# A schedule's leads by block, and second-layer weights left until block 3

## The chip, the cores and the metric
One core of a Trainium2 chip runs the whole program. The metric is the device time in microseconds (us), the median of several runs. TensorE does the matrix products and takes its instructions in order; ScalarE and VectorE move results out of the accumulators and do all arithmetic by element, each in its own order; SP issues the transfers between memories, also in order, and waits with the whole queue where one transfer has to wait.

## What is computed
Three stages follow each other: a scan with decay over 768 positions of 4 x 8 heads, and two layers of two products each.
```python
def _attn_ref(x, a, B, C):          # chunks of 32 positions
    ...
        L = np.exp(cum[:, :, :, None] - cum[:, :, None, :])
        L = L * causal
        M = np.einsum('bhin,bhjn->bhij', Cc, Bc) * L
        y[:, :, sl] = M @ xc + (Cc @ state) * np.exp(cum)
        state = decay_full * state + sum_j(Bc[j] * xc[j] * decay_from_j)
    ...
def _moe_ref(x, w_in, w_out):       # first layer, 3072 x 256 -> 2048 -> 256
    h = x @ w_in
    return np.maximum(0.01 * h, h) @ w_out
def _moe2_ref(x, w_in, w_out):      # second layer, the same sizes
    h = np.maximum(x @ w_in, 0.0)
    return h * h @ w_out
```
(The lines of the scan are shortened.) The result is 3072 tokens x 256 numbers in float32.

## The kernel before
**The scan** runs over 12 pieces of 256 positions, counted from 0 here as in the code; three pieces in a row are one sequence of the batch. `scan_a` (L356) and `scan_b` (L401) are generators that emit a step at each `yield`. For one piece they make, in this order: scales of its inputs (for later sequences from sums of squares over `all` loads, L307), the half-precision parts `him`, `ch`, `xh`, `cl`, `kmx`, `xl`, two decay scans `le` (L229, L234), the products S from `kbd` (32 columns wide, L388), `mkh` and `mkl`, the products Y from `xbh` and `xbl` (48 columns wide, L417 to L419), the state scan `stt` (L251), its halves `shl` and their transpose `t` (L426 to L430), the products Y from `sbd` (32 columns, L438), and at last `yh` and `yl` (L447, L448), which are the first layer's input. `kbd`, `xbh`, `xbl` and `sbd` are block-diagonal operands, each put together by four transfers that SP issues (`diag`, L348).

**The first layer** (class `One`) runs over 9 blocks, `BLOCKS`: six of one piece, three of two pieces. A block has 16 column groups of 128 hidden units; a step takes two of them (`hmm` into `hp`, 12 products of 256 columns), `act` makes `g` in two halves, and `omm` adds a step's share to the output `oo` two or three steps later (12 products). Block 0 works in plain single precision on weights as they come (`raw`); block 1 and later use each weight and input as a sum of two parts, three products for one.

**Weights** come as 64-bit floats. A chunk is loaded into `wst` (L122), turned into 32-bit numbers by two ScalarE instructions (L131, L134) and two VectorE ones (L142 and L147 or L151), and split into two parts, one instruction on each engine (L173, L174). There are 16 chunks for the first layer (`w1i`, `w1o`) and 16 for the second (`w2i`, `w2o`), in the order of the list `wq`. `raw_step` (L186) moves chunks on in blocks before and during block 0, `w_one` (L194) does one step of one chunk afterwards; the variable `acc` says how often (L721).

**The order.** One loop (L698) goes through all steps of the nine blocks; a step counts as two columns in the position `pos`. After each step, `stages_to(due(pos + 2))` (L708) emits as many steps of the scan as are due there: stage k holds the first half of piece k and the second half of piece k - 1, and `starts` (L673) says which stage has to be reached how many columns ahead of each block. Between, the due stage rises by `RATE` per column. The build then sets each engine's instructions in an order that follows the emission but isn't equal to it; that order is fixed in the program.

**The second layer** (class `Two`, L555) follows with six groups of two pieces, 512 columns a product.

Of the kernel before, what the change touches and what calls it, by code (L numbers as in the profile page):

```python
# [38 lines left out]
LAG2 = 2  # L39
W_AHEAD = 4  # L40
RATE = 1.4 / KO
LEAD = 4
NSTEP = 15
APART = 3
PRE = 8
# [9 lines left out]
def ssd_moe_kernel(ctx: ExitStack, tc: tile.TileContext, in1, in2, w1i, w1o, w2i, w2o, out):  # L55
# [52 lines left out]
    wq = [(nm, c) for k in range(10) for nm, c in (("1i", k), ("1o", k - 2)) if 0 <= c < 8]  # L108
    wq += [(nm, c) for nm in ("2i", "2o") for c in range(8)]
    w_loaded, w_half, w_full = [], [], []  # L110
    w_raw, pair = {}, {}

    def load_w():
        nm, c = wq.pop(0)
        st = big([P, 2, 256], I64, "wst", "st", 7)
        if nm[1] == "i":
            src = w_dram[nm][:, :, c * 256 : c * 256 + 256]
        elif nm == "1o":
            src = w_dram[nm][:, 2 * c : 2 * c + 2, :]
        else:  # L120
            src = w_dram[nm][:, c :: KO // 2, :]
        nc.sync.dma_start(st, src)  # L122
        w_loaded.append((nm, c, st))

    def split_w():
        nm, c, st = w_loaded.pop(0)
        v = st.bitcast(I32).rearrange("p k (f two) -> p k f two", two=2)
        w0, w1 = v[:, :, :, 0], v[:, :, :, 1]


        nc.scalar.activation(w1.bitcast(F32), w1.bitcast(F32), AF.Copy, scale=2.0**-112)  # L131


        nc.scalar.activation(  # L134
            w0, w0.bitcast(U32), AF.Copy, scale=2.0**-29 * (1 - 2.0**-14), bias=7.5 * 2.0**-14 - 0.5
        )
        w_half.append((nm, c, w0, w1))

    def split_w1():

        nm, c, w0, w1 = w_half.pop(0)
        nc.vector.scalar_tensor_tensor(w0, w1, 3, w0, ALU.logical_shift_left, ALU.bitwise_or)  # L142
        if nm[0] == "1":
            if c % 2 == 0:
                pair[nm] = big([P, 2, 2, 256], F32, "raw", *RAW[nm])
            w = w_raw[nm, c] = pair[nm][:, c % 2]
            nc.vector.scalar_tensor_tensor(w.bitcast(I32), w1, -(1 << 31), w0, ALU.bitwise_and, ALU.bitwise_or)  # L147
            w_full.append((nm, c, w))
            return
        if nm != "2o":  # L150
            nc.vector.scalar_tensor_tensor(w0, w1, -(1 << 31), w0, ALU.bitwise_and, ALU.bitwise_or)  # L151
            w_full.append((nm, c, w0.bitcast(F32)))
            return
        a = big([P, 8, P], F32, "wa", "st", 7)
        nc.vector.scalar_tensor_tensor(
            a[:, 0:4].rearrange("p (k d) f -> p k (d f)", k=2).bitcast(I32),
            w1, -(1 << 31), w0, ALU.bitwise_and, ALU.bitwise_or,
        )
        nc.vector.scalar_tensor_tensor(a[:, S1], a[:, 0], -1.0, a[:, A22], ALU.mult, ALU.subtract)
        nc.vector.tensor_tensor(a[:, S3], a[:, A11], a[:, 0], ALU.subtract)  # L160
        nc.vector.scalar_tensor_tensor(a[:, S2], a[:, S1], -1.0, a[:, A11], ALU.mult, ALU.subtract)
        nc.vector.tensor_tensor(a[:, S4], a[:, A12], a[:, S2], ALU.subtract)
        w_full.append((nm, c, a[:, 1:8]))

    def split_w2():

        nm, c, w = w_full.pop(0)
        if nm == "2o":
            h, l = w_done[nm, c] = tuple(big([P, 7, P], F32R, x) for x in ("wh", "wl"))
        else:  # L170
            t = w_done[nm, c] = big([P, 2, 2, 256], F32R, f"w{nm}")
            h, l = t[:, 0], t[:, 1]
        nc.scalar.activation(h, w, AF.Copy)  # L173
        nc.vector.tensor_tensor(l, w, h.bitcast(F32), ALU.subtract)  # L174
# [9 lines left out]
            load_w()  # L184

    def raw_step():  # L186
        if w_half and w_half[0][0][0] == "1":
            split_w1()
        if w_loaded:
            split_w()  # L190
        if wq and len(w_loaded) < W_AHEAD:
            load_w()

    def w_one():  # L194
# [256 lines left out]
    blocks, q0 = [], 0  # L451
# [96 lines left out]
    def split_y(g):  # L548
        y = yf.pop(g)
        h, l = (big([P, 2, KI, TP], F32R, t, "y", 4) for t in ("xh", "xl"))  # L550
        nc.scalar.copy(h, y)
        nc.vector.tensor_tensor(l, y, h.bitcast(F32), ALU.subtract)
        ys[g] = h, l
# [104 lines left out]
    def stages_to(x):  # L658
        while now[0] < NP + 1 and now[0] + min(now[1] / (2 * NSTEP if now[0] <= APART else NSTEP), 0.99) < x:
            k = next(sc_it, NP + 1)  # L660
            now[:] = (k, now[1] + 1) if k == now[0] else (k, 0)
# [3 lines left out]
    for _ in range(PRE):  # L665
        raw_step()
# [3 lines left out]
    for i, (p0, n) in enumerate(blocks):  # L670
        todo += [(i, list(range(m, m + 2 // n))) for m in range(0, KO, 2 // n)]
    at_ = [2 * [i for i, _ in todo].index(i) for i in range(len(blocks))]
    starts = [(at - LEAD, p0 + n + (0.5 if p0 + n <= APART else 1)) for at, (p0, n) in list(zip(at_, blocks))[1:]]  # L673

    def due(at):
        return max(nb - max(RATE * (b - at), 0) for b, nb in starts)
# [3 lines left out]
    def second(lag):  # L680
        while len(pend) > lag:
            ph_, ms, end = pend.pop(0)
            ph_.omm(ms)
            if end:
                ph_.finish()
# [5 lines left out]
    def need_raw(nm, c):  # L691
        while (nm, c) not in w_raw:
            raw_step()

    pos = 0
    acc = 0.0
    ones_ = {}
    for i, ms in todo:  # L698
        p0, n = blocks[i]
        m = ms[0]  # L700
        if i not in ones_:
            ones_[i] = One(p0, n)
        ph_ = ones_[i]
        (need_raw if i == 0 else need)("1i", m // 2)
        ph_.hmm(ms)
        pos += 2
        ph_.act(ms)
        stages_to(due(pos + 2))  # L708
        pend.append((ph_, ms, ms[-1] == KO - 1))
        if len(pend) > LAG[n]:  # L710
            (need_raw if pend[0][0].f32 else need)("1o", pend[0][1][-1] // 2)
        second(LAG[n])
        if i == 0:
            if any(v[0] == "1" for v, *_ in wq + w_loaded + w_half):
                raw_step()
                raw_step()
            if m >= 4:
                split_w2()
        else:
            first_w = w_full and w_full[0][0][0] == "1"  # L720
            acc += 1.5 if first_w else (0.3 if i < len(blocks) - 1 else 1.5)  # L721
            while acc >= 1:
                acc -= 1
                (split_w2 if first_w else w_one)()
                first_w = w_full and w_full[0][0][0] == "1"
        if i == len(blocks) - 1 and m == KO - 4:
            split_y(0)
        if ms[-1] == KO - 1 and p0 % 2 + n == 2:
            ys.pop(p0 // 2)
# [68 lines left out]
```

## Time and profile before
| | |
|---|---|
| median of 3 runs | 616.76 us (616.14 to 616.87) |
| profiled execution | 616.98 us |
| its span, first to last instruction | 615.2 us |
| TensorE busy | 574.8 us (93%) |
| VectorE busy | 457.6 us (74%) |
| ScalarE busy | 444.5 us (72%) |
| chain that ended last | TensorE 77%, ScalarE 11%, VectorE 6%, transfers 3% |

Times in the profile are counted from the first instruction. The busy time of TensorE is modelled at the ends of products, and two products that follow each other overlap in the rows; the distance of their starts is what one costs. A share of the whole span hides that the stretches differ: the table by stage in the rows below does not.

### The profile page before, as it was taken

To read this page: it belongs to the slowest core of one execution; us is meant where nothing else is said; L and a number is where in the kernel's file an instruction comes from. 1 tells how busy PE (TensorE), PEld (TensorE's weight loads), DVE (VectorE), ACT (ScalarE), POOL (GpSimd) and SP (SyncE) were. 2 spreads that over 40 slices of the span, in tenths; PEclk is the share of its full clock that TensorE was granted. 3 is DMA by queue.
4 is the path that set the end of the run, shared out by engine and by line. 5 is a ranking of instruction groups with operands and counts; after the bars stand their busy time and mean duration, and the time that the engine had idled before them with its cause. 6 is when DMAs were issued, how large, how long until landed. Compare 5 with 4: busy or idle time off the path is not lost.

```text
span 615.2 us, 11663 instructions
## 1 busy us (share of the span) xinstructions
PE 574.8 (93%) x4610; PEld 518.3 (84%) x4610; DVE 457.6 (74%) x774; ACT 444.5 (72%) x715; POOL 5.2 (1%) x15
## 2 busy tenths in 40 slices
PE   0399985999999999999999999999999999999996
PEld 0388885999999978888888889989999999999996
DVE  6999997676687878655756467887787877776765
ACT  6999976656856866556656578878778778777773
POOL 3000000000000000000000000000000000000000
PEclk9999996999999999999999999999999999999999
DMA  8864873557355752111301000010010000100101
GB/s 290 288 175 143 286 198 40 115 127 236 45 110 115 253 101 54 15 23 41 111 1 34 1 0 2 2 36 0 1 36 1 9 27 2 36 1 0 35 1 35
DMA packets 113574, 46.50 MB, mean 76 GB/s; under 512 B 94448, under 2 KB 103280, under 8 KB 113520
## 3 DMA queue, kind: packets, MB, share of 16 engines
q1 hardware_dynamic: 113520, 45.76, 27.5%
q8 instruction: 36, 0.59, 0.4%
q14 instruction: 18, 0.15, 0.1%
HBM read 36.83 MB, written 3.15 MB: 65 GB/s over the span
## 4 chain that ended last, share of the span: by engine, by line
PE 77%; ACT 11%; DVE 6%; DMA 3%; issue 1%; SPq 1%; DVEq 0%; ACTq 0%
PE hp L469 13%; PE hp L470 12%; PE hp L471 12%; PE o L531 4%; PE o L610 4%; PE o L537 4%; PE o L532 4%; PE o L608 4%; PE o L609 3%; PE Ym L610 3%; PE Ym L609 3%; PE Ym L608 3%; PE oo L537 2%; ACT wst L131 2%; PE oo L532 2%; PE oo L531 2%
## 5 line engine op out<-in xcount | busy, mean ns | idle before, releaser
L508 DVE TENSOR_TENSOR g<-t,g 128x512 fp32r<-128x512 f32 x88 | 60.4, 688 | 53.4 <-ACT t L507 53.0
L586 DVE TENSOR_TENSOR tl<-ts,th 128x1024 fp32r<-128x1024 f32 x48 | 58.8, 1225 | 47.2 <-ACT th L584 47.2
L506 ACT ACTIVATE g<-hp 128x512 fp32r<-128x512 f32 x88 | 52.4, 596 | 49.4 <-PE o L537 32.9
L469 PE MATMUL hp<-yl,w1i 128*128 128x256 f32 (+1 forms) x256 | 84.4, 330 | 1.1 <-DVE yl L448 1.1
L471 PE MATMUL hp<-yh,w1i 128*128 128x256 f32 (+1 forms) x256 | 84.0, 328 | 0.0
L470 PE MATMUL hp<-yh,w1i 128*128 128x256 f32 (+1 forms) x256 | 83.9, 328 | 0.0
L574 ACT ACTIVATE b<-hp 128x512 f32<-128x512 f32 x96 | 57.1, 595 | 32.7 <-PE hp L471 32.7
L469 PE MATMUL hp<-xl,w2i 128*128 128x512 f32 x192 | 75.3, 392 | 0.0
L470 PE MATMUL hp<-xh,w2i 128*128 128x512 f32 x192 | 75.2, 392 | 0.0
L471 PE MATMUL hp<-xh,w2i 128*128 128x512 f32 x192 | 74.7, 389 | 0.0
L584 ACT CAST th<-ts 128x1024 fp32r<-128x1024 f32 x48 | 50.3, 1048 | 17.8 <-DVE ts L583 17.7
L469 PEld LDWEIGHTS hp<-yl,w1i 128*128 128x128 f32 x256 | 49.7, 194 | 5.3 <-DVE yl L448 1.5
L471 PEld LDWEIGHTS hp<-yh,w1i 128*128 128x128 f32 x256 | 49.7, 194 | 3.7
L470 PEld LDWEIGHTS hp<-yh,w1i 128*128 128x128 f32 x256 | 49.7, 194 | 3.6
L507 ACT ACTIVATE t<-hp 128x512 f32<-128x512 f32 x88 | 52.3, 594 | 0.0
L575 ACT ACTIVATE b<-b 128x1024 f32<-128x1024 f32 x48 | 50.9, 1061 | 1.1
L585 DVE TENSOR_TENSOR bl<-b,bh 128x768 fp32r<-128x768 f32 x48 | 45.7, 952 | 0.0
L581 DVE TENSOR_TENSOR ts<-b 128x512 f32<-128x512 f32 x48 | 33.1, 691 | 14.3 <-ACT b L575 13.6
L471 PEld LDWEIGHTS hp<-xh,w2i 128*128 128x128 f32 x192 | 36.1, 188 | 7.9
L469 PEld LDWEIGHTS hp<-xl,w2i 128*128 128x128 f32 x192 | 36.2, 189 | 6.4
L580 ACT CAST bh<-b 128x768 fp32r<-128x768 f32 x48 | 40.2, 837 | 1.3
L470 PEld LDWEIGHTS hp<-xh,w2i 128*128 128x128 f32 x192 | 36.2, 189 | 5.8
(167 smaller groups left out, 1570.5 us busy)
## 6 DMA issues: line engine op xcount, KB each, us to landing
in<-in SPq DMA_DIRECT2D x12, 640.0 KB, 4.9
in<-in SPq DMA_DIRECT2D x12, 512.0 KB, 5.3
all<-in SPq DMA_DIRECT2D x15, 384.0 KB, 6.3
wst<-w1i SPq DMA_DIRECT2D x8, 512.0 KB, 6.9
wst<-w1o SPq DMA_DIRECT2D x8, 512.0 KB, 5.9
wst<-w2i SPq DMA_DIRECT2D x8, 512.0 KB, 7.0
wst<-w2o SPq DMA_DIRECT2D x8, 512.0 KB, 4.4
out_t<-r SPq DMA_DIRECT2D x24, 128.0 KB, 1.7
```

The source lines that it names most:

```text
L469: nc.tensor.matmul(hp, wh[:, k, c], xl[:, :, k], start=(k == 0), stop=False)
L470: nc.tensor.matmul(hp, wh[:, k, c], xh[:, :, k], start=False, stop=False)
L471: nc.tensor.matmul(hp, wl[:, k, c], xh[:, :, k], start=False, stop=(k == KI - 1))
L506: nc.scalar.activation(g[:, 0], hp, AF.Lrelu)
L507: nc.scalar.activation(t, hp, AF.Lrelu)
L508: nc.vector.tensor_tensor(g[:, 1], t, g[:, 0].bitcast(F32), ALU.subtract)
L574: nc.scalar.activation(b[:, 2 * i : 2 * i + 2], hp.rearrange("p (n t) -> p n t", n=2), AF.Relu)
L575: nc.scalar.activation(b, b, AF.Square)
L584: nc.scalar.copy(th, t)
L585: nc.vector.tensor_tensor(bl, b[:, 1:], bh.bitcast(F32), ALU.subtract)
L586: nc.vector.tensor_tensor(tl, t, th.bitcast(F32), ALU.subtract)
L608: nc.tensor.matmul(o, wl[:, s], h[:, i], start=first and new, stop=False, skip_group_check=True)
```

## The change
`LEAD`, one number before, becomes a list with an entry for each block: the scans for blocks 2 to 6 are due 8, 8, 6, 4 and 2 columns sooner than before, those for the other blocks as before. `raw_step` loads first-layer chunks alone and no longer stops at `W_AHEAD` chunks in flight. In the loop `w_one` is not called for second-layer weights in blocks 0 to 2 (`W2_FROM = 3`); from block 3 to 7 its share per step rises from 0.3 to 0.4.
```diff
 LAG2 = 2
 W_AHEAD = 4
 RATE = 1.4 / KO
-LEAD = 4
+LEAD = [0, 4, 12, 12, 10, 8, 6, 4, 4]
+W2_FROM = 3
 NSTEP = 15
 APART = 3
 PRE = 8
@@ -184,11 +185,11 @@
             load_w()
 
     def raw_step():
-        if w_half and w_half[0][0][0] == "1":
+        if w_half:
             split_w1()
         if w_loaded:
             split_w()
-        if wq and len(w_loaded) < W_AHEAD:
+        if wq[0][0][0] == "1":
             load_w()
 
     def w_one():
@@ -670,7 +671,9 @@
     for i, (p0, n) in enumerate(blocks):
         todo += [(i, list(range(m, m + 2 // n))) for m in range(0, KO, 2 // n)]
     at_ = [2 * [i for i, _ in todo].index(i) for i in range(len(blocks))]
-    starts = [(at - LEAD, p0 + n + (0.5 if p0 + n <= APART else 1)) for at, (p0, n) in list(zip(at_, blocks))[1:]]
+    starts = [
+        (at - lead, p0 + n + (0.5 if p0 + n <= APART else 1)) for at, lead, (p0, n) in list(zip(at_, LEAD, blocks))[1:]
+    ]
 
     def due(at):
         return max(nb - max(RATE * (b - at), 0) for b, nb in starts)
@@ -718,7 +721,7 @@
                 split_w2()
         else:
             first_w = w_full and w_full[0][0][0] == "1"
-            acc += 1.5 if first_w else (0.3 if i < len(blocks) - 1 else 1.5)
+            acc += 1.5 if first_w else 0 if i < W2_FROM else (0.4 if i < len(blocks) - 1 else 1.5)
             while acc >= 1:
                 acc -= 1
                 (split_w2 if first_w else w_one)()
```
VectorE, around the masked product `in` of piece 2 (out of S, for which `in_374` is the buffer) and its rest `mkl`, before; `wst` and `w2i` are second-layer weights here, `in_747` is piece 3:
```order
L151 SCALAR_TENSOR_TENSOR wst<-wst 128x512
L174 TENSOR_TENSOR w2i<-wst,w2i 128x512
L142 SCALAR_TENSOR_TENSOR wst<-wst 128x512
L508 TENSOR_TENSOR g<-t,g 128x512
L174 TENSOR_TENSOR w2i<-wst,w2i 128x512
L151 SCALAR_TENSOR_TENSOR wst<-wst 128x512
L398 SCALAR_TENSOR_TENSOR in_374<-S,kk,le 128x16x32
L142 SCALAR_TENSOR_TENSOR wst<-wst 128x512
L229 SCALAR_TENSOR_TENSOR le<-in_747,delta 128x512
L234 SCALAR_TENSOR_TENSOR le<-in_747,d1e 128x512
L151 SCALAR_TENSOR_TENSOR wst<-wst 128x512
L409 TENSOR_TENSOR mkl<-in_374,mkh 128x768
```
The same place in the changed kernel (the lines count one more; `raw`, `w1i` and `w1o` are first-layer weights, `in_692` is piece 3):
```order
L175 TENSOR_TENSOR w1i<-raw,w1i 128x512
L509 TENSOR_TENSOR g<-t,g 128x512
L175 TENSOR_TENSOR w1o<-raw,w1o 128x512
L175 TENSOR_TENSOR w1i<-raw,w1i 128x512
L509 TENSOR_TENSOR g<-t,g 128x512
L175 TENSOR_TENSOR w1o<-raw,w1o 128x512
L399 SCALAR_TENSOR_TENSOR in_374<-S,kk,le 128x16x32
L547 COPY yf<-oo 128x256
L230 SCALAR_TENSOR_TENSOR le<-in_692,delta 128x512
L410 TENSOR_TENSOR mkl<-in_374,mkh 128x768
```
The second-layer weights are gone from there, and splits of the first layer's weights stand ahead and behind instead; `mkl` follows `in` after two instructions, not after four.

SP, from the last first-layer loads to the block-diagonal operands of piece 2, before (`t_625` is piece 1's transpose, `in_746` and `in_747` are piece 3):
```order
L122 DMA wst<-w1o 128x512 x3
L122 DMA wst<-w2i 128x2x256 x2
L352 DMA sbd<-t_625 32x16x32 x4
L122 DMA wst<-w2i 128x2x256 x2
L314 DMA all<-in 128x3x256 x2
L215 DMA in_746<-in 128x1280
L216 DMA in_747<-in 128x1024
L122 DMA wst<-w2i 128x2x256 x2
L352 DMA kbd<-kmx 32x16x32 x4
L314 DMA all<-in 128x3x256 x2
L352 DMA xbh<-xh 32x16x32 x4
```
SP in the changed kernel, the same place (`t_577` is piece 1's transpose, `in_691` and `in_692` are piece 3):
```order
L123 DMA wst<-w1o 128x512
L315 DMA all<-in 128x3x256
L123 DMA wst<-w1o 128x512 x2
L353 DMA sbd<-t_577 32x16x32 x4
L315 DMA all<-in 128x3x256
L216 DMA in_691<-in 128x1280
L217 DMA in_692<-in 128x1024
L353 DMA kbd<-kmx 32x16x32 x4
L315 DMA all<-in 128x3x256 x2
L353 DMA xbh<-xh 32x16x32 x4
```
The loads `w2i` are gone, and the first `all` load stands ahead of the last two of the first layer and of piece 1's `sbd`.

TensorE, behind the last product with `sbd` of piece 2, before:
```order
L439 LDWEIGHTS sbd
L439 MATMUL Y<-ql,sbd 128x32
L388 LDWEIGHTS kbd
L388 MATMUL S<-ch,kbd 128x32
L389 LDWEIGHTS kbd
```
TensorE in the changed kernel, the same place:
```order
L440 LDWEIGHTS sbd
L440 MATMUL Y<-ql,sbd 128x32
L532 MATMUL oo<-g,w1o 128x256
L533 MATMUL oo<-g,w1o 128x256
L532 MATMUL oo<-g,w1o 128x256
L533 MATMUL oo<-g,w1o 128x256
L538 MATMUL oo<-g,w1o 128x256 x4
```
Before, the products S of piece 3 follow at once; now 20 output products of block 1 stand between. The same holds ahead of the `sbd` products: 26 products of block 1 stood between the 48-column products of piece 2 and these, and 73 do now.

## Rows read from the trace of the kernel before
**Rows 1.** Timeline, TensorE: start us, us, what, count [idle before <- releaser].
```profile
64.47 0.39 PE L469 MATMUL hp<-yl,w1i 128*128 128x256 f32 x1 [1.11 <-DVE yl L448]
...
84.42 0.18 PE L418 MATMUL Y<-mkl,xbh 128*128 128x48 f16 x1 [1.54 <-DVE mkl L409]
...
97.60 0.19 PE L438 MATMUL Y<-qh,sbd 128*128 128x32 f16 x1 [4.98 <-DMA sbd<-t]
...
100.47 0.18 PE L388 MATMUL S<-ch,kbd 128*128 128x32 f16 x1 [1.86 <-DMA kbd<-kmx]
...
222.67 0.47 PE L531 MATMUL o<-g,w1o 128*128 128x512 f32 x1 [1.33 <-DVE yf L546]
```

**Rows 2.** Busy time by stage: stretch and its length, then us busy by engine.
```profile
29.00:64.50 35.50, 33.80 (x241) 28.63 (x241) 34.39 (x69) 34.09 (x67) 0.00 (x0) 1.00 0.60 180
64.50:92.70 28.20, 26.57 (x278) 26.10 (x278) 27.34 (x53) 23.69 (x48) 0.00 (x0) 1.00 0.75 226
92.70:101.40 8.70, 1.94 (x65) 1.89 (x65) 5.82 (x13) 4.94 (x10) 0.00 (x0) 0.69 0.33 39
...
110.00:205.00 95.00, 94.83 (x1204) 94.02 (x1201) 68.65 (x120) 60.93 (x118) 0.00 (x0) 1.00 0.57 140
205.00:240.00 35.00, 33.67 (x320) 28.87 (x320) 29.22 (x57) 24.98 (x46) 0.00 (x0) 1.00 0.49 114
```

**Rows 3.** The same, products into `hp` alone: TensorE us (count), granted clock.
```profile
101.33:106.00 4.67, 4.67 (x21) 0.50 0.39 46
107.00:108.33 1.33, 1.33 (x11) 1.00 0.43 49
```

**Rows 4.** Groups of VectorE, 64 to 97 us, and two of its timeline.
```profile
L151 DVE SCALAR_TENSOR_TENSOR wst<-wst 128x512 int32<-128x512 int32 x6 | 4.1, 687 | 0.0
L142 DVE SCALAR_TENSOR_TENSOR wst<-wst 128x512 int32<-128x512 int32 x6 | 4.0, 688 | 0.0
...
L174 DVE TENSOR_TENSOR w2i<-wst,w2i 128x512 fp32r<-128x512 f32 x4 | 2.7, 688 | 0.0
...
88.50 0.69 DVE L151 SCALAR_TENSOR_TENSOR wst<-wst 128x512 int32<-128x512 int32 x1
89.10 0.69 DVE L142 SCALAR_TENSOR_TENSOR wst<-wst 128x512 int32<-128x512 int32 x1
```

**Rows 5.** Timeline of ScalarE, VectorE and SP (SPq), piece 2's state.
```profile
89.03 0.48 ACT L421 ACTIVATE d1s<-Y,kk 128x256 f32<-128x256 f32 x1 [0.47 <-PE Y L419]
...
90.51 0.75 DVE L251 TENSOR_TENSOR_SCAN stt<-dec,d1s 128x288 f32<-128x288 f32 x1
...
92.67 0.71 DVE L430 STREAM_TRANSPOSE t<-shl 128x512 f16<-128x512 f16 x1
...
93.45 2.61 SPq L352 DMA_DIRECT2D sbd<-t  x4
```

**Rows 6.** Timeline of VectorE and TensorE, end of block 0.
```profile
55.14 0.71 DVE L430 STREAM_TRANSPOSE t<-shl 128x512 f16<-128x512 f16 x1
...
60.15 0.18 PE L438 MATMUL Y<-qh,sbd 128*128 128x32 f16 x1
...
60.95 2.40 PE L525 MATMUL oo<-g,raw 128*128 128x256 f32 x10
...
63.66 0.75 DVE L448 SCALAR_TENSOR_TENSOR yl<-Y,fac,yh 128x512 fp32r<-128x512 f32 x1
```

**Rows 7.** Timeline of VectorE, piece 2's `mkl`.
```profile
83.42 0.96 DVE L409 TENSOR_TENSOR mkl<-in,mkh 128x768 f16<-128x768 f32 x1
```

**Rows 8.** Timeline of SP, ahead of piece 2's `kbd`.
```profile
62.55 5.57 SPq L122 DMA_DIRECT2D wst<-w2i  x2
```

**Rows 9.** Transfers into `kbd`, 60 to 130 us.
```profile
DMA to landing us min/median/max: 2.0/2.0/5.8
```

**Rows 10.** Timeline of VectorE, piece 7's `yl` and block 5's copy.
```profile
203.73 0.74 DVE L448 SCALAR_TENSOR_TENSOR yl<-Y,fac,yh 128x512 fp32r<-128x512 f32 x1
...
222.11 0.41 DVE L546 COPY yf<-oo 128x256 f32<-128x256 f32 x1
```

## The prediction
> **What bounds the kernel now.** I read the waits of TensorE first, since the page has it busy for 93% of the span and 77% of the chain that ended last. After its first product of block 0 it waits five times for 1 us or more [rows 1]: 1.1 us for `yl` of piece 1, 1.5 us for `mkl` of piece 2, 5.0 us for the `sbd` transfers of piece 2, 1.9 us for the `kbd` transfers of piece 3, and 1.3 us at the start of block 6. The table by stage comes next [rows 2]: TensorE is filled from 110 to 205 us (94.8 of 95), in the stretch from 92.7 to 101.4 it works 1.9 of 8.7 us. VectorE is the reverse: 34.4 of 35.5 and 27.3 of 28.2 us until 92.7, 68.7 of 95 later. So the kernel is bound by VectorE (with ScalarE close to it) until piece 2 has its `y`, and by TensorE from there on. What is late at 92.7 can be bought back only before 92.7.
>
> A loss that no wait shows is in the clock: the granted clock is 0.50 in the first products of block 2, 21 of which take 4.67 us, 0.222 each; with the clock at 1.00 11 of them take 1.33 us, 0.121 each [rows 3]. Those are the two levels of 1.2 and 2.4 GHz, and the fall came in the stretch in which TensorE did nearly nothing [rows 2]. It costs 21 x (0.222 - 0.121) = 2.1 us, with the product that straddles the rise some 2.3.
>
> **What the change moves, part by part.** *Second-layer weights.* Between 64 and 97 us VectorE does 6 + 6 + 4 = 16 instructions on the second layer's first weights, 0.69 us each, of which the next one starts 0.60 later, since their ends overlap (88.50 and 89.10 [rows 4]): 9.6 us. In the new order none stands there. ScalarE loses its share of them in the same way, and SP the six loads. They come back in blocks 3 to 7, beside TensorE at 94.8 of 95 us, where VectorE has 95 - 68.7 = 26 us free [rows 2]: I cost them at nothing there; without that cover they would cost up to the 9.6 us that they take.
>
> *Piece 2's scan.* Of what VectorE does ahead of the transpose `t` of piece 2, the 16 weight instructions and three subtractions of `g` (0.60 each) go behind it, 19 x 0.60 = 11.4 us. VectorE being filled to there, `t` can come 11.4 us sooner. Ahead of its `mkl` 10 weight instructions of the second layer, 4 of the first, 3 of `g` and one scan of 1.13 go: also 11.4 us.
>
> What TensorE waits for is a chain [rows 5]: the 48-column products of piece 2 end at 89.0, then `d1s`, the scan `stt`, `shl`, `t` at 92.7, four issues at SP from 93.45, landing, and the product starts at 97.6 [rows 1]: 8.6 us. In the order of before 26 products of block 1 (3.1 us) and the scale product (0.3) stand between; 8.6 - 3.4 = 5.2 is the wait of 5.0. In the new order the 48-column products are set far earlier, and 36 `hp` and 37 `oo` products stand between: 73 x 0.12 + 0.3 = 9.0 us. That covers the chain by 0.4 us, with little to spare. I take **5.0 us gained** (bounds: 5.0, and 2.4 if the chain is 3 us longer).
>
> *Piece 3's `kbd`.* Its four issues follow piece 2's `sbd` at SP, 2.6 us later [rows 5], and TensorE came to them at once. Now 20 `oo` products (2.4 us) stand between, and the landing is 0.4 us ahead to begin with. **1.9 us gained** (bounds 1.0 and 1.9). The same 20 products and the 32 of S cover the 2.2 us in which `yh` and `yl` of piece 2 are made. Without idle time before block 2, the clock should not fall: **2.3 us gained** (bounds 0 and 2.3).
>
> *Start of block 1.* `t` of piece 1 moves 1.5 us sooner on VectorE (55.1 to 53.7 [rows 6]), but in TensorE's order its product Y moves four single-precision `oo` products sooner, 4 x 0.43 = 1.7 us (5 of them, recorded as 10, took 2.40 with the tail [rows 6]): from 60.2 to 58.4, or 58.6 when the transfers land. `yl`, which ended at 64.4 [rows 6], has 1.8 us less ahead of it on VectorE, and `yh` less on ScalarE, where however the cast `shl` now stands before `stt` is done and waits about 1.3 us. So `yl` ends between 62.6 and 64.4; I take 63.1. Block 1 then starts 1.3 us sooner, owing four products of block 0 that it did not owe, 1.7 us: **0.4 us lost** (bounds: 0.1 gained, 1.7 lost).
>
> *Piece 2's `mkl` at TensorE.* From block 1's start at 63.1, 61 products of 0.12, 5 of 0.43 and S (1.0) come first: TensorE gets to it at 73.6. `mkl` started at 83.4 and took 0.96 [rows 7], so it can end at 73.0. **1.5 us gained, 0.3 lost again**, since anything late on either side shows (bounds 0 and 1.5 lost again).
>
> *What may stand in the way at SP.* `kbd` of piece 2 was issued behind two loads of second-layer weights that held SP for 5.6 us [rows 8]. They are gone, and an `all` load and piece 3's two loads stand ahead of it now: issued about 59.0 to 61.6. A landing takes 2.0 us in the median and 5.8 at most [rows 9]: 63.6 or 67.4. TensorE comes to S of piece 2 at 63.1 + 2.9 + 2.2 = 68.2. The slower one is covered by 0.8: I take 0 (bounds: 0, and 1.9 lost, the wait that a late `kbd` of piece 3 made [rows 1]).
>
> *Pieces 3 to 6.* Their products are set sooner in TensorE's order as well. Between the 48-column products and the `sbd` products of a piece stand 14 us or more of TensorE's work from piece 3 on, against the chain of 8.6; `mkl` of piece 3 is the close one (S to Y of 3.4 us against 3.5 for the four VectorE steps between). 0.3 us lost (bounds 0 and 3).
>
> *Start of block 6.* TensorE waits for VectorE's copy `yf` of block 5 [rows 1]; between `yl` of piece 7 (203.7) and that copy (222.1) VectorE does 18.4 us [rows 10]. In the new order 15.1 us of instructions stand there, but Y of piece 7 is set 27 products (3.2 us) later: the wait stays as it is, 0 (bounds 1.3 gained, 2 lost). From the later half of block 6 on the two orders hold the same work in the same places, and TensorE is the bound: what is gained stays.
>
> **The sum.** 5.0 + 1.9 + 2.3 + 1.5 = 10.7 gained; 0.4 + 0.3 + 0.3 = 1.0 lost. The profiled execution took 616.98 (span 615.2 and 1.8 around it), 0.2 over the median of the runs: 616.98 - 9.7 = 607.3, and as a median **607.1 us**.
>
> **Rivals.**
> A. *Piece 2's `sbd` stays late.* For: the cover of 0.4 us is thin, and ScalarE, which takes part in the chain twice, has a sum of squares before it that waits for an `all` load. Against: the load is issued some 15 us sooner than it was. If the chain is 3 us longer, 2.6 us of wait remain. In the trace the clock is at half behind the waits of 5.0 and 1.9 us, which stand close together, and at full behind those of 1.1 and 1.5 [rows 1, 3]; a single wait of 2.6 is not in it. If the clock stays up, 609.7 comes out, if it falls as before, 607.1 + 2.6 + 2.3 = 612.0; I take the second. The Trainium skill is on that side: in TensorE: Matmul & The Clock Gate, section Loop structure matters more than you think, a wait for a DMA between runs of products lets the clock drop to half, and the products behind it run cold. The rows agree with it for the long wait and have nothing on one of this size.
> B. *Given back later.* The weight work, put into blocks 3 to 7, delays `g` or `yf` there. For: VectorE is at 29.2 of 35 us at 205 to 240 [rows 2], and TensorE does wait for it there. Against: 26 us are free at 110 to 205. With 2 us more at block 6 and 1.5 at blocks 3 to 5: 610.6.
> C. *Slower.* The products S and Y of pieces 2 to 6 now stand further ahead in TensorE's queue, which takes them in order; where their `kbd` or `sbd` has not landed, all `hp` and `oo` products behind wait too. With the 1.9 us of `kbd` and 1.5 us of `mkl` at each of five pieces, 17 us are lost against 10.7 gained: 623. It decides from 2.1 us a piece. Against: TensorE waits for none of these between 110 and 205 now (94.8 of 95 us [rows 2]), and the new places leave 3 us and more but for those named.
> D. *No change.* If VectorE's total, which stays the same, were the bound through block 5, moving it would not help: 616.8. Against: 26 us idle there.
>
> **Chances.** Forecast 0.63, A 0.15, B 0.15, C 0.04, D 0.03. Runs of this kernel differ by 0.1%, so 0.2% (1.2 us) is what can be told from none: faster 0.93, same 0.03, slower 0.04. The range goes from everything gained with the wait at block 6 gone too (616.8 - 10.7 - 1.3 = 604.8) to rival A: 604.5 to 612.0. The forecast's own range is 605 to 609.5.
>
> **What the profile would show.** If right: no wait of TensorE over 1 us between 65 and 110 us; the first products of block 2 at 91 to 92.5 instead of 101.3, at 0.12 us each, and no slice with a clock under 9 after the first; no second-layer weight work on VectorE before about 110; `t` of piece 2 at 81 to 82; a wait of about 1.3 us, 10 us sooner, at block 6. Rival A shows as a wait for `sbd` and a half clock near 87, B as waits for `g`, `yf` or `mkl` between 95 and 230, C as waits at five pieces. The forecast is wrong if block 2 starts later than 95, or if it starts at 92 and the end does not follow.

## The result, and the profile after

| | before | after |
|---|---|---|
| median on one chip | 616.51 us (616.14 to 616.87) | 606.37 us (605.52 to 606.47) |
| ratio | | 0.9827, 95% interval 0.9807 to 0.9847 |
| profiled execution | 616.98 us | 606.45 us |
| its span | 615.2 us | 604.7 us |

The forecast was 607.1. A later run of the same kernel (e9_changed_again) gave 0.9819 (0.9803 to 0.9834).

The timeline of TensorE in the changed kernel, the places that answer to [rows 1] (lines count one more): start us, us, what, count, and in brackets the idle time before and what ended it. Rows without a bracket were not waited for: S of piece 2 at 68.43, its first 48-column product at 73.75, its first `sbd` product at 87.52, S of piece 3 at 90.81, the start of block 2 at 91.63.
```profile
58.45 1.10 PE L526 MATMUL oo<-g,raw 128*128 128x256 f32 x4 [0.88 <-DVE raw L148]
...
63.31 0.39 PE L470 MATMUL hp<-yl,w1i 128*128 128x256 f32 x1 [0.71 <-DVE yl L449]
...
64.84 0.60 PE L526 MATMUL oo<-g,raw 128*128 128x256 f32 x2
...
66.70 1.89 PE L526 MATMUL oo<-g,raw 128*128 128x256 f32 x8
68.43 0.18 PE L389 MATMUL S<-ch,kbd 128*128 128x32 f16 x1
...
73.75 0.20 PE L418 MATMUL Y<-mkh,xbh 128*128 128x48 f16 x1
...
87.52 0.19 PE L439 MATMUL Y<-qh,sbd 128*128 128x32 f16 x1
...
90.81 0.19 PE L389 MATMUL S<-ch,kbd 128*128 128x32 f16 x1
...
91.63 0.36 PE L470 MATMUL hp<-yl,w1i 128*128 128x256 f32 x1
...
95.33 0.18 PE L419 MATMUL Y<-mkl,xbh 128*128 128x48 f16 x1 [0.35 <-DVE mkl L410]
...
212.19 0.47 PE L532 MATMUL o<-g,w1o 128*128 128x512 f32 x1 [1.30 <-DVE yf L547]
```
The waits of 1.5, 5.0 and 1.9 us are gone. Between 64 and 205 us one wait of 0.35 is the longest. The wait at block 6 has kept its size and stands 10.5 us sooner. New is a wait of 0.88 in block 0 for first-layer weights (`raw`).

The table by stage, columns as in [rows 2] (busy us and count of TensorE, weight loads, VectorE, ScalarE, GpSimd, then granted clock, share of transfers, GB/s):
```profile
64.50:92.70 28.20, 28.20 (x340) 27.67 (x339) 24.66 (x50) 21.75 (x43) 0.00 (x0) 1.00 0.57 138
92.70:101.40 8.70, 8.35 (x122) 8.11 (x121) 8.28 (x13) 6.34 (x13) 0.00 (x0) 1.00 0.50 105
...
110.00:205.00 95.00, 95.00 (x1147) 93.75 (x1146) 74.06 (x134) 68.54 (x131) 0.00 (x0) 1.00 0.60 154
205.00:240.00 35.00, 33.70 (x323) 27.57 (x321) 30.88 (x56) 26.08 (x49) 0.00 (x0) 1.00 0.56 123
```
TensorE is now full from 64.5 to 205 us but for that 0.35, VectorE has 3.5 us free in the stretch in which it had 0.9. At 110 to 205 us VectorE carries 5.4 us more than before, beside a TensorE that is full: the weight work went where it costs nothing. The products into `hp` at the start of block 2, alone (stretch, its length, busy us and count, granted clock), against 0.50 in [rows 3]:
```profile
91.50:95.00 3.50, 3.24 (x24) 1.00 0.43 51
```
And the chain of piece 2's state, which [rows 5] shows of before, with its `mkl` (from the timelines of ScalarE, VectorE and SP):
```profile
71.81 0.93 DVE L410 TENSOR_TENSOR mkl<-in,mkh 128x768 f16<-128x768 f32 x1
...
78.65 0.47 ACT L422 ACTIVATE d1s<-Y,kk 128x256 f32<-128x256 f32 x1
...
79.53 0.75 DVE L252 TENSOR_TENSOR_SCAN stt<-dec,d1s 128x288 f32<-128x288 f32 x1
...
81.69 0.71 DVE L431 STREAM_TRANSPOSE t<-shl 128x512 f16<-128x512 f16 x1
...
82.47 2.62 SPq L353 DMA_DIRECT2D sbd<-t  x4
```
`t` comes 11.0 us sooner (92.67 before). From `d1s` to the issue the chain takes 3.8 us (4.4 before), so it is hardly shorter; TensorE has other products to do meanwhile.

### The profile page after: what moved, and what is told of

It reads as the page before. It is cut to its first block, busy times and chain, and to the rows that moved or that the text cites. A ratio compares the mean times of both kernels' runs of the same rounds, so it can differ in the third digit from the quotient of the medians.

```text
span 604.7 us, 11654 instructions
## 1 busy us (share of the span) xinstructions
PE 572.1 (95%) x4610; PEld 516.3 (85%) x4610; DVE 455.6 (75%) x774; ACT 445.5 (74%) x715; POOL 5.2 (1%) x15
## 4 chain that ended last, share of the span: by engine, by line
PE 86%; DVE 7%; ACT 4%; issue 2%; DMA 1%; DVEq 0%; ACTq 0%
PE hp L470 13%; PE hp L471 13%; PE hp L472 13%; PE o L532 4%; PE o L611 4%; PE o L538 4%; PE o L533 4%; PE o L609 4%; PE o L610 4%; PE oo L533 3%; PE oo L538 3%; PE oo L532 3%; PE Ym L611 3%; PE Ym L610 3%; PE Ym L609 3%
## 5 line engine op out<-in xcount | busy, mean ns | idle before, releaser
L471 PE MATMUL hp<-yh,w1i 128*128 128x256 f32 (+1 forms) x256 | 83.2, 325 | 0.0
L472 PE MATMUL hp<-yh,w1i 128*128 128x256 f32 (+1 forms) x256 | 83.0, 324 | 0.0
L472 PEld LDWEIGHTS hp<-yh,w1i 128*128 128x128 f32 x256 | 48.7, 190 | 3.7
L471 PEld LDWEIGHTS hp<-yh,w1i 128*128 128x128 f32 x256 | 48.7, 190 | 3.7
```

What stands on the lines that cost most here:

```text
L471: nc.tensor.matmul(hp, wh[:, k, c], xh[:, :, k], start=False, stop=False)
L472: nc.tensor.matmul(hp, wl[:, k, c], xh[:, :, k], start=False, stop=(k == KI - 1))
```

## The experiments

Three theories stood beside each other: VectorE's weight work in block 1 was the bound and its going is the gain; the leads make the gain; withholding `w_one` makes it. The first four runs take the parts of the change one by one.

**e1_weights_only**
```diff
-LEAD = [0, 4, 12, 12, 10, 8, 6, 4, 4]
+LEAD = [0, 4, 4, 4, 4, 4, 4, 4, 4]
```


> The changed kernel with all leads back at 4 columns: only the second-layer weights are left alone. Theory 1 (what binds block 1 is VectorE, and the weight work is what has to leave it): nearly the whole gain stays. In its order piece 2's t stands 12.0 us of VectorE work sooner than before and 70 products stand between the 48-column and the sbd products of piece 2, so the waits of 5.0, 1.9 and 1.5 us and the half clock go; yl of piece 1 stands 1.9 us later, but block 0 then owes 3 output products and not 10, 7 x 0.43 = 3.0 us. 607.0 us, 606 to 609. Theory 2 (the leads make the gain): the scan stays due as late as before, only the 1.5 us of mkl go, 615 us.

Measured: 608.25 us, 0.9871 (0.9853 to 0.9888). The wait at block 1 (timeline of TensorE), and `hp` products behind it (columns as above, granted clock after the count):
```profile
66.01 0.35 PE L470 MATMUL hp<-yl,w1i 128*128 128x256 f32 x1 [2.98 <-DVE yl L449]
```
```profile
66.00:69.50 3.50, 2.77 (x14) 0.62 0.74 96
```
Most of the gain stays, as Theory 1 has it; none of the three later waits is there. What the expectation had not counted is the clock: behind a single wait of 3 us at block 1 it falls. The 0.62 is the mean of a stretch with both levels: its first six products start 0.12 us apart, the others 0.21.

**e2_leads_only** (the kernel before, with the list)
```diff
-LEAD = 4
+LEAD = [0, 4, 12, 12, 10, 8, 6, 4, 4]
```


> The kernel before with the list of leads alone; second-layer weights as before. Theory 1 (VectorE binds block 1): a part of the gain. The scan of piece 2 is set ahead of weight work (t 7.2 us of work sooner), so the sbd wait goes, but the weight work then stands ahead of yl of piece 2, which comes 2.9 us of work sooner only. Block 2 starts at 95.5 to 98 in the place of 101.3: 3.5 to 6 us gained up to there; the clock may or may not fall in the wait for yl that takes the others' place. 611 us, 608.5 to 613. Theory 2 (the leads make the gain): 606 to 607.

Measured: 613.23 us, 0.9946 (0.9934 to 0.9958), just over the range of Theory 1 and far from Theory 2. TensorE's waits between 70 and 200 us, and the clock of all its products behind the second and the third:
```profile
82.94 0.39 PE L329 MATMUL S<-mx,ones 128*128 128x3 f32 x2 [0.99 <-ACT sq L274]
...
95.69 0.54 PE L470 MATMUL hp<-yl,w1i 128*128 128x256 f32 x1 [1.19 <-DVE yl L449]
...
125.81 0.20 PE L418 MATMUL Y<-mkh,xbh 128*128 128x48 f16 x1 [2.24 <-DVE yl L449]
```
```profile
95.60:98.50 2.90, 2.81 (x13) 0.53 1.04 252
...
127.50:130.00 2.50, 2.50 (x46) 0.52 0.22 34
```
Block 2 starts at 95.7, as expected (95.5 to 98): the `sbd` wait is gone, and `yl` behind the weight work sets the start. The 2.2 us of `yl` at 125.8 were not foreseen, nor that the clock falls behind both waits.

**e3_raw_only** (the kernel before, with this edit alone)
```diff
-        if w_half and w_half[0][0][0] == "1":
+        if w_half:
...
-        if wq and len(w_loaded) < W_AHEAD:
+        if wq[0][0][0] == "1":
```


> The kernel before with raw_step alone changed (no second-layer chunk is loaded or worked on in it); leads 4, w_one from block 1 on at 0.3. Theory 1: the sixteen weight instructions of 64 to 97 us came from the chunks that raw_step had loaded ahead, so this part alone makes most of the gain; w_one brings some work back into block 2, where yl of piece 2 is 8.8 us of VectorE work sooner and not 10.6. 607.5 us, 606.5 to 609.5. Theory 2 (leads): 615 to 616.5. Theory 3 (withholding w_one in blocks 0 to 2 makes the gain): 615 to 616.5.

Measured: 610.13 us, 0.9893 (0.9878 to 0.9907), above the range by 0.6. The wait at block 1 and the `hp` products behind it:
```profile
66.55 0.55 PE L470 MATMUL hp<-yl,w1i 128*128 128x256 f32 x1 [2.92 <-DVE yl L449]
```
```profile
66.50:72.40 5.90, 5.14 (x22) 0.50 0.69 113
```
The two edited lines make 1.07% of the 1.7% that the whole change makes; the half clock lasts 5.9 us here, which the expectation had left out. Theories 2 and 3 fall as the main cause.

**e4_from_only** (the kernel before, with this edit alone)
```diff
-            acc += 1.5 if first_w else (0.3 if i < len(blocks) - 1 else 1.5)
+            acc += 1.5 if first_w else 0 if i < W2_FROM else (0.4 if i < len(blocks) - 1 else 1.5)
```


> The kernel before with W2_FROM = 3 and the share of 0.4 alone; raw_step and the leads as before. The order up to piece 4 is that of before, so Theory 1 expects no change: 616.5 us, 615.8 to 617.3, with the waits of 1.5, 5.0 and 1.9 us and the half clock all there. Theory 3 (withholding w_one in blocks 0 to 2 makes the gain): 607 to 609.

Measured: 616.86 us, 1.0003 (0.9993 to 1.0014). Theory 3 falls: the waits of before are all there (timeline of TensorE; the one for `kbd` is 1.85 us).
```profile
85.10 0.18 PE L419 MATMUL Y<-mkl,xbh 128*128 128x48 f16 x1 [1.60 <-DVE mkl L410]
98.27 0.18 PE L439 MATMUL Y<-qh,sbd 128*128 128x32 f16 x1 [4.98 <-DMA sbd<-t]
```

**e5_leads_and_raw** (the changed kernel with)
```diff
-W2_FROM = 3
+W2_FROM = 0
...
-            acc += 1.5 if first_w else 0 if i < W2_FROM else (0.4 if i < len(blocks) - 1 else 1.5)
+            acc += 1.5 if first_w else 0 if i < W2_FROM else (0.3 if i < len(blocks) - 1 else 1.5)
```


> The changed kernel without its third part: w_one for second-layer weights again from block 1 on at 0.3 (W2_FROM = 0). Against the changed kernel this gives what withholding w_one is worth, against e3_raw_only what the leads are worth. Block 1 starts as in the changed kernel (a wait of about 0.7 us, clock up), where e3_raw_only waits 2.9 us and falls to half clock. yl of piece 2 stands 1.8 us of VectorE work later than in the changed kernel, which costs about 1 us at the start of block 2. Theory 1 (VectorE binds until block 2): 607.5 us, 606.5 to 609. If the leads are worth nothing beside the weights: 610, as e3_raw_only.

Measured: 606.99 us, 0.9831 (0.9818 to 0.9844), not to be told from the changed kernel. The wait at block 1:
```profile
63.59 0.39 PE L470 MATMUL hp<-yl,w1i 128*128 128x256 f32 x1 [0.77 <-DVE yl L449]
```
Against e3_raw_only (0.9893), the leads are worth 0.6%, 3.8 us: without them block 1 waits 2.9 us and goes on at half clock, with them 0.8 and at full clock (1.00 from 63.5 to 67 us). By share of the time before, the two parts nearly add up: leads 0.54%, `raw_step` 1.07%, together 1.69%.

**e6_weights_off_block5** (the changed kernel with)
```diff
-            acc += 1.5 if first_w else 0 if i < W2_FROM else (0.4 if i < len(blocks) - 1 else 1.5)
+            acc += 1.5 if first_w else (0, 0, 0, 0.7, 0.7, 0, 0.4, 0.4, 1.5)[i]
```


> The changed kernel with the share of w_one by block: 0.7 in blocks 3 and 4, none in block 5, then 0.4 as before. The wait of 1.3 us at the start of block 6 is put down to VectorE, filled from 195 to 212 us with weight work among the scan's; between yl of piece 7 and the copy yf of block 5 stand 11.6 us of VectorE work in this order, 15.1 in the changed kernel. If that is the cause, the wait goes and 605.1 us comes out, 604.7 to 605.9. If the wait is set elsewhere (the scan of piece 8, ScalarE), it stays: 606.4. If 0.7 is too much for blocks 3 and 4, waits appear between 120 and 170 us: over 607.

Measured: 606.73 us, 0.9820 (0.9807 to 0.9833): no difference from the changed kernel that can be told.
```profile
213.07 0.47 PE L532 MATMUL o<-g,w1o 128*128 128x512 f32 x1 [0.81 <-DVE yf L547]
```
The wait shrinks from 1.30 to 0.81 and does not go. The edit does not take all weight work from there: between `yl` of piece 7 and the copy `yf` VectorE still does three weight instructions, seven in the changed kernel. So how much of the wait is weight work stays open.

**e7_longer_chain** (the changed kernel with)
```diff
-        nc.vector.tensor_tensor(shl[:, :, :, 1, :], sv, shl[:, :, :, 0, :], ALU.subtract)
+        for _ in range(6 if p == 2 else 1):
+            nc.vector.tensor_tensor(shl[:, :, :, 1, :], sv, shl[:, :, :, 0, :], ALU.subtract)
```


> The changed kernel with the subtraction that makes the second half of shl done six times for piece 2 alone (the same values), which puts 5 x 0.6 = 3 us of VectorE work into the chain ahead of its t. The build answers by putting S of piece 3 ahead of the sbd products and piece 2's t 5.6 us of work later. t then ends at 87.9 and the sbd products can start at about 92.6 in the place of 87.5, block 2 at about 95.9 with nothing owed of block 1, where 93.3 would do: 2.6 us of wait. If a wait of that size leaves the clock up: 609.0 us. If the clock falls to half as in e1_weights_only and e3_raw_only: 611.0, up to 611.5. If the slack ahead of block 2 were as large as 3 us: 606.5.

Measured: 609.55 us, 0.9864 (0.9848 to 0.9880). Timeline of TensorE (lines count one more again), `hp` products behind the first wait, and all products behind the second:
```profile
95.96 0.18 PE L418 MATMUL Y<-mkh,xbh 128*128 128x48 f16 x1 [1.64 <-DVE yl L450]
...
216.78 0.47 PE L533 MATMUL o<-g,w1o 128*128 128x512 f32 x1 [1.84 <-DVE yf L548]
```
```profile
95.90:98.30 2.40, 2.29 (x13) 0.63 0.43 52
```
```profile
216.70:219.00 2.30, 2.22 (x10) 1.00 0.37 43
```
The slack ahead of block 2 is less than 3 us. The wait is 1.6, not 2.6, and it is for `yl`, not for `sbd`. Against the changed kernel 0.4% is lost (0.9864 and 0.9827), 2.3 us. In the profiled execution, of 611.10 us, the clock falls behind the wait and nowhere else from 29 us on, which makes a mean of 0.997 over the span. The other three runs took 610.63, 608.48 and 608.48 us at means of 0.997, 1.000 and 0.999. So by these means the clock fell in two runs of four, and those took 2.4 us longer. Both branches of the expectation came out, 609.0 and 611.0, and the median of 609.55 lies between the two.

**e8_more_lead** (the changed kernel with)
```diff
-LEAD = [0, 4, 12, 12, 10, 8, 6, 4, 4]
+LEAD = [0, 4, 16, 16, 14, 12, 8, 4, 4]
```


> The changed kernel with leads of 16, 16, 14, 12 and 8 columns for blocks 2 to 6 (12, 12, 10, 8 and 6 in the changed kernel). S and the 48-column products of piece 2 stand right behind piece 1's sbd products in TensorE's order, before block 0 is done, 10 us of TensorE work sooner; VectorE gets to mkl of piece 2 only 5.2 us sooner. Theory of rival C (products of the scan set too far ahead hold up all that is queued behind them): waits of 3 to 6 us for kbd and mkl of piece 2 between 58 and 70 us and a fall of the clock, 609 to 613 us. If more lead does no harm: 606.4 or a little under.

Measured: 620.18 us, 1.0043 (1.0030 to 1.0056): slower than the kernel before, and worse than expected. TensorE, SP and VectorE, from their timelines:
```profile
59.19 0.21 PE L439 MATMUL Y<-qh,sbd 128*128 128x32 f16 x1 [3.80 <-DMA sbd<-t]
...
69.58 2.05 PE L493 MATMUL hp<-y,raw 128*128 128x256 f32 x4 [8.49 <-DVE raw L148]
...
57.78 0.63 SPq L353 DMA_DIRECT2D kbd<-kmx  x1
...
59.12 0.61 SPq L123 DMA_DIRECT2D wst<-w1i  x1
...
68.75 1.29 DVE L148 SCALAR_TENSOR_TENSOR raw<-wst 128x512 int32<-128x512 int32 x2
```
More lead does harm, but TensorE does not wait for `kbd` and `mkl` of piece 2: in SP's order piece 2's `kbd` and piece 1's `sbd`, which have to wait for VectorE's `kmx` and `t`, stand ahead of the last first-layer loads, the weights of block 0 are late, and its products wait 8.5 us for them.

**e9_changed_again** (no edit)

> The changed kernel itself, to stand beside the next two on the same chip: 0.983 of the kernel before (606.4 at 616.5), with a wait of 1.3 us at the start of block 6.

Measured: 605.88 us, 0.9819 (0.9803 to 0.9834), with a wait of 1.31 at the start of block 6.

**e10_best** (e6_weights_off_block5 with)
```diff
-                (nc.scalar.copy if d == 0 else nc.vector.tensor_copy)(to[:, :, d], o)
+                (nc.scalar.copy if d == 0 or self.p0 == 5 else nc.vector.tensor_copy)(to[:, :, d], o)
```


> As e6_weights_off_block5, and in block 5 both halves of the copy yf are made by ScalarE. There the wait at the start of block 6 fell to 0.8 us only, with VectorE's half of yf at 212.5 to 212.9 and ScalarE's at 211.0 to 211.4; a second one of 0.3 on ScalarE ends at 211.7, before TensorE gets to it at 212.3. The wait goes: 1.3 us less than the changed kernel, 0.981 of the kernel before (604.9 at 616.5). If the wait then falls on something else (g, the state's halves on ScalarE), no difference from the changed kernel that can be told.

Measured: 605.19 us, 0.9807 (0.9792 to 0.9823); span 603.3 against 604.4 of e9_changed_again. ScalarE's two copies, and the product that had waited for them:
```profile
209.98 0.65 ACT L547 COPY yf<-oo 128x256 f32<-128x256 f32 x2
...
210.88 0.40 PE L532 MATMUL o<-g,w1o 128*128 128x512 f32 x1
```
The wait is gone and 1.1 us of the span with it, so it was for VectorE to get to its half of the copy. By the medians it is 0.7 us (605.88 - 605.19), and the intervals overlap: the lowest of all times, but not shown to beat the changed kernel.

**e11_lead14** (the changed kernel with)
```diff
-LEAD = [0, 4, 12, 12, 10, 8, 6, 4, 4]
+LEAD = [0, 4, 14, 14, 12, 10, 8, 4, 4]
```


> The changed kernel with leads of 14, 14, 12, 10 and 8 columns for blocks 2 to 6, half-way to e8_more_lead. Theory from e8_more_lead (more lead does harm through SP's order: piece 2's kbd, which has to wait for kmx, is set ahead of the last first-layer loads, and block 0's products wait for the weights that come from them): here the last two of these loads, and not four, stand behind piece 2's kbd, so a wait for raw of 3 to 6 us and a half clock behind it: 0.990 of the kernel before, 0.986 to 0.997 (610 at 616.5). If the harm came from VectorE's order (yl of piece 1 stands 2.0 us of work later than in the changed kernel, in e8_more_lead 0.8): a wait for yl of about 2 us and none for raw, 0.986.

Measured: 609.33 us, 0.9876 (0.9860 to 0.9893), which both theories reach; the wait decides (TensorE, then VectorE):
```profile
64.78 0.35 PE L470 MATMUL hp<-yl,w1i 128*128 128x256 f32 x1 [3.80 <-DVE yl L449]
...
63.88 0.75 DVE L449 SCALAR_TENSOR_TENSOR yl<-Y,fac,yh 128x512 fp32r<-128x512 f32 x1
```
It is for `yl` of piece 1, and none is for `raw`: here VectorE's order does the harm, and SP's theory, which held for e8_more_lead, does not. The time is that of e1_weights_only (0.9871): two columns more take back all that the leads are worth.

## Why the prediction was right

**VectorE as the bound until piece 2.** Shown: taking its sixteen weight instructions away (e3_raw_only) removes the waits of 5.0 and 1.5 us and the half clock at block 2, and leaves 0.5 of the 1.9 for `kbd`, with the old leads. That run takes ScalarE's share and SP's loads away too, and no run parts the three; that VectorE's queue was the late one rests on rows of before (timelines of ScalarE and VectorE):
```profile
81.54 0.82 ACT L404 CAST mkh<-in 128x768 f16<-128x768 f32 x1
...
82.83 0.67 DVE L151 SCALAR_TENSOR_TENSOR wst<-wst 128x512 int32<-128x512 int32 x1
...
89.83 0.69 DVE L151 SCALAR_TENSOR_TENSOR wst<-wst 128x512 int32<-128x512 int32 x1
```
ScalarE's `mkh` is done at 82.4, and VectorE starts `mkl` at 83.42 [rows 7], right behind a weight instruction; `d1s` is done at 89.5, and `stt` starts at 90.51 [rows 5], when another has ended. The work came from chunks that `raw_step` had loaded ahead; withholding `w_one` (e4_from_only, e5_leads_and_raw) has no effect that can be measured. The prediction had not said which of the two edits it was.

**The terms.** The 5.0, 1.9 and 1.5 us went as priced. `mkl` ended at 72.7 and TensorE came to it at 73.75 (forecast 73.0 and 73.6); `t` started at 81.7 (81 to 82), the `sbd` products at 87.5 (about 87), block 2 at 91.6 (91 to 92.5), where it owes the last 12 output products of block 1 (1.4 us), which were done by then before. The 2.3 us of the clock came back too. The pieces after cost 0.35 (forecast 0.3), the start of block 6 nothing (1.33 and 1.30). The 0.3 that `mkl` of piece 2 was to lose again was not lost.

**Start of block 1.** Forecast 0.4 us lost, measured 0.6: it starts 1.16 us sooner (64.47 and 63.31) and owes five single-precision products (recorded as 2 and 8) where it owed one, 4 x 0.43 = 1.7. The wait of 0.88 us for `raw` ahead of it was not forecast; by the rows it did not make `yl` later, since VectorE works without a gap from 57.6 us to `yl` (62.51 to 63.26, forecast 63.1). The step was right in size, but the prediction did not see what it guards: with the old leads the same place has a wait of 2.9 to 3.0 us and a half clock (e1_weights_only, e3_raw_only). This is where the leads earn most of theirs.

**The sum.** 10.7 - 0.6 - 0.35 = 9.8 by these rows; the two profiled executions differ by 10.5, the medians by 10.1. Of the 0.7 left, 0.2 are small waits of the kernel before (94.83 of 95 us busy at 110 to 205, 95.00 after); the rest has no row of its own. The 9.8 lies within the interval of the ratio (9.4 to 11.9 us).

**The rivals.** A: `sbd` of piece 2 was in time. Of the two prices that it had for the clock it chose the fall; behind the 1.6 us of e7_longer_chain the clock fell in two runs of four. The Trainium skill (TensorE: Matmul & The Clock Gate, section Loop structure matters more than you think) has the clock drop to half in a wait for a transfer between products. Its example waits 8 us, and here a wait of 1.2 us, for VectorE, was followed by 0.53 (e2_leads_only). B: no wait at blocks 3 to 5 over 0.35, none longer at block 6. C: not at these leads; at two columns more (e11_lead14) 3.5 us are lost (609.33 - 605.88), at four (e8_more_lead) all of the gain and more, through block 0's weights and piece 1's `yl` and not through `kbd` and `mkl` of later pieces. D: refuted.

## What to carry to other kernels

Where one engine is full early and has room later, work that nobody needs yet is worth moving even if its total stays: here the gain was the waits of the bound engine behind it, and the half clock behind these. Look for who emits the work: the loading ahead in `raw_step` did it, not the loop that is meant to pace it. Setting a chain sooner pays until it passes work that the running block still needs; two columns further the sign of the step turned.

## What was not expected of the hardware

The clock fell behind short waits too, not only behind the long one: behind 1.2 us (e2_leads_only, 0.53 in the stretch after) and behind 2.9 and 3.0 us at block 1 (0.50 and 0.62), and behind 1.6 us (e7_longer_chain, 0.63) in two runs of four. Other waits left it at 1.00: those of 1.1, 1.5 and 1.3 us in the kernel before, and at block 6 one of 1.8 us in e7_longer_chain and one of 2.8 us in e8_more_lead (timeline of TensorE, and all products behind it):
```profile
226.79 0.47 PE L532 MATMUL o<-g,w1o 128*128 128x512 f32 x1 [2.77 <-DVE yf L547]
```
```profile
226.80:230.00 3.20, 3.20 (x14) 1.00 0.40 46
```
So the length of a wait alone does not say whether the clock falls. Nor does a row of 32-column products of the scan ahead: directly ahead of the 1.2 us stand 32 of them, but ahead of the 2.8 us too, with two products of 512 columns between. What decides is not shown here. A wait behind which it falls can cost about twice what its row shows: behind the 2.9 us of e3_raw_only, 22 products took 5.14 us at 0.50, where 0.12 each would make 2.6.
